# Fused attention and gated-GELU block on one core: the opening reordered around the values' weights

## The chip, the cores and the metric

The kernel runs on one core of one Trainium2 chip. The core has five engines that work side by side and meet at semaphores: TensorE (PE; its weight loads are shown apart as PEld), VectorE (DVE), ScalarE (ACT), GpSimd (POOL) and SyncE (SP, which only issues transfers here). Each engine takes its own instructions strictly in the order in which the program wrote them; one that waits holds up everything behind it on that engine. The metric is the device time of one execution in microseconds (us), the median of several.

## The reference

```python
x = A_x                                              # 1 x 2048 x 576
xn = layernorm(x)                                    # over the last axis
qkv = (xn @ wqkv).reshape(B, S, 3, 32, 18)           # 32 heads of 18
p = softmax(q @ k^T * 18 ** -0.5)
s = (p @ v).reshape(B, S, 576) @ wo
h = gelu_tanh(xn @ w_gate) * (xn @ w_up)             # 576 -> 4608
g = silu(h @ w_down)                                 # 4608 -> 576
return x + s * g
```

Everything is float32. The kernel keeps that accuracy with float16 products: each operand is split into a high and a low half (`XH`, `XL` for the normalized input; `w.hi`, `w.lo` for weights), and a product is the sum of high by high, high by low and low by high.

## The kernel before, in words

The 2048 rows are 16 tiles of 128 rows; the 576 columns are four blocks of 128 and one of 64 (the last block's high and low halves lie together in `XT`). The program has an opening, a first loop, and a long main loop.

**Weights.** `prep` turns one block of weights into its halves. Its steps are: load; largest magnitude of each of five row blocks (`amax`, DVE); the largest over all partitions (`par` to `top`); a power of two from it (`power`, `floor`, `inverse`, DVE); high halves (`split_hi`, ACT, L330); low halves (`split_lo`, on DVE where `urgent`, else on POOL). With `urgent` the largest over the partitions goes over two tiny PE products (L271, L282); otherwise it goes out to DRAM (`mxd`, L274) and comes back spread to all partitions (`mb`, L289). There is one `prep` for each of five head sets of seven heads (`j0` to `j4`, queries and keys together), one for the values (`v`), one for each of 18 gate chunks (`c0` to `c17`) and one for the output weights. The blocks that are not urgent are queued as pieces in `bg`; `subtick` takes up to three of them whenever the program calls it, as long as a budget of ACT, DVE and POOL time for that step allows.

**The opening (L1171 to L1251).** For each tile: statistics on DVE (`ln_stats`, for two or four tiles at a time, with one square root on ACT, L1141, and five small DVE steps); normalization on DVE (`ln_norm`, L1150), high half on ACT (L1154), low half on POOL (L1155, L1156); nine transpositions on PE (`ln_tr`, L1162) into PSUM (`s1` and `s2` in turn), and two copies on ACT (`ln_out`, L1167, L1168) into `XHT` and `XL`. Behind each tile stands `proj_fine`: the product of the head set `j0` with this one tile, 28 products of 128 columns (L412 to L415). After every fourth tile `evac_j` takes the two finished PSUM tiles to float16 halves (`evh` on ACT, `evl` on DVE) and stores them to DRAM in head order (`KD` from SP, `QD` from POOL for `j0`). The values' weights are loaded when tile 5 has its turn, and their pieces are dealt out over the later tiles by `V_PLAN`. After the last tile the preparations of `j1` and `c0` are queued.

**The first loop (L1442 to L1465).** `load_qk(0)` reads the first pair of heads back from DRAM (`KT`, `QT`, L1257, L1258). `qk1(0, k)`, for k from 0 to 63, is a product of one query tile with 512 keys for both heads (L1274, two matmuls that run together) and the largest of each row (L1277, DVE). Between these products PE is filled: first by the value products (`unit_v`: per tile two halves of 14 products of 288 columns, L487 to L492, taken from PSUM by ACT, L598, and stored by POOL, L612), then by `g_run`, which takes slots of a stream of paired products. A pair is 27 slots, and a slot is two matmuls on the two halves of the PE rows (L468). `pairs` gives the order of that stream: `j1`, `c0`, `c1`, `j2`, `c2`, `c3`, `j3`, and so on. 

**The main loop (from L1488).** For each of 16 pairs of heads there are 64 steps. A step has one product of the second kind (`qk2`, L1326) with its exponential (L1332), one `qk1` of the next pair, and a share of the stream's slots, of down products (L728, twelve matmuls to a stage) or of the products of probabilities and values (L1351), dealt out by `make_plan` so that all of the stream's slots are gone by the end of pair 14. Every row of `order` named below is a row of the built program.

The lines that the prediction follows most closely are these:

```python
order = [("v", spec_v) ...]                  # the stream's order
for j in units_j:
    order += [j, units_c.pop(0), units_c.pop(0)]
...
load_qk(0)
fills(9, 2.0)
while k < 64:
    if done_units[0]: qk1(0, k); subtick(FIRST); g_run(7); ...
    else:             qk1(0, k); qk1(0, k + 1); ...; fill(1.9)
```

## Time and profile before

| | |
|---|---|
| median of 3 runs | 2615.22 us (2613.48 to 2615.82) |
| the profiled execution | 2615.07 us, of which the span from first to last instruction 2613.3 us |
| busy share of the span | PE 96%, DVE 74%, ACT 64%, POOL 58% |
| first product of the first loop that has both heads | 93.98 us |
| last of its 64 products | 194.58 us |
| sixth product of the second pair (from here the main loop runs) | 216.20 us |

In the views below a row of the timeline has the start in us, the duration in us, the engine, the line, the operation, output and inputs, and in square brackets the idle time ahead of it with what ended it. Rows that PE overlaps are pipelined: the distance of two starts, not the duration, is what one matmul costs. A row of a window table has the stretch, its length, the busy time of PE, PEld, DVE, ACT and POOL with their instructions, the granted PE clock (1.00 is full speed), the busy share of the DMA engines and GB/s.

### The profile page before, as it was taken

The page shows a single profiled execution, that of the slowest core. Times are in us where ns is not written, and L with a number is a line of the kernel's source. Part 1 is how long each engine was busy: PE and PEld are TensorE (multiplying, and loading weights), DVE is VectorE, ACT ScalarE, POOL GpSimd, SP SyncE. Part 2 cuts the span into 40 slices and gives each one's busy share as a digit, 9 for nine tenths or more (in the row PEclk, how much of TensorE's full clock was granted, in tenths as well). Part 3 has the DMA queues.
Part 4 walks back from the last instruction along what each step waited for, and adds up shares of the span by engine and source line. Part 5 has one row for each costly group of instructions (what it writes and reads, how often), then busy time and mean ns, then how long its engine had stood idle before and what let it go on. Part 6 is the DMA issues. An engine that isn't in the chain of part 4 may idle for free.

```text
span 2613.3 us, 60781 instructions
## 1 busy us (share of the span) xinstructions
PE 2509.3 (96%) x25800; PEld 1326.2 (51%) x25800; DVE 1933.6 (74%) x2719; ACT 1661.2 (64%) x2081; POOL 1509.2 (58%) x1428
## 2 busy tenths in 40 slices
PE   6899999999999999999999999999999999999987
PEld 6564545455545545455555455555445444445544
DVE  7587778777877777777777778787777777777544
ACT  5225666666767666766666666767666675666663
POOL 4247663576537553757656574847666675847413
PEclk9999999999999999999999999999999999999999
DMA  4430022201120112101011120201111111100123
GB/s 144 124 113 16 12 58 63 53 18 54 34 79 19 33 31 64 45 24 51 13 53 25 23 55 11 56 9 39 28 36 26 37 29 40 38 19 6 45 72 123
DMA packets 134156, 118.68 MB, mean 45 GB/s; under 512 B 60160, under 2 KB 112792, under 8 KB 133884
## 3 DMA queue, kind: packets, MB, share of 16 engines
q1 hardware_dynamic: 128892, 105.38, 15.0%
q0 software_dynamic: 2432, 6.54, 0.7%
q8 instruction: 201, 3.29, 0.5%
q10 hardware_dynamic: 2560, 2.89, 0.3%
q14 instruction: 71, 0.58, 0.1%
HBM read 84.89 MB, written 29.61 MB: 44 GB/s over the span
## 4 chain that ended last, share of the span: by engine, by line
PE 79%; DVE 10%; ACT 4%; issue 2%; DMA 2%; POOL 2%; SPq 0%; ACTq 0%; POOLq 0%; DVEq 0%
PE mb_t L468 16%; PE ma_t L468 15%; PE md_t L728 15%; PE md_t L1351 9%; PE s L1326 8%; PE s L1274 8%; PE ma_t L1351 6%; DVE PM L1277 3%; ACT P L1332 1%; DVE osb L1359 1%; DVE m_c L248 1%; PE md_t L900 1%; PE mb_t L900 1%; PE mb_t L1351 1%; DMA QT<-QD 1%
## 5 line engine op out<-in xcount | busy, mean ns | idle before, releaser
L1277 DVE TENSOR_REDUCE PM<-s 128x2 f32<-128x1024 f32 x1024 | 1251.1, 1224 | 341.1 <-PE s L1274 332.7
L1332 ACT ACTIVATE P<-s,etab 128x1024 f32<-128x1024 f32 x896 | 996.1, 1112 | 620.5 <-PE s L1326 605.0
L468 PE MATMUL ma_t<-XHT,whi_c 64*128 64x512 f16 x1440 | 542.4, 377 | 10.5 <-DVE osb L1357 5.6
L468 PE MATMUL mb_t<-XHT,whi_c 64*128 64x512 f16 x1440 | 542.3, 377 | 3.8 <-DVE touch L436 2.0
L468 PE MATMUL ma_t<-XHT,wlo_c 64*128 64x512 f16 x1296 | 487.9, 376 | 0.0
L468 PE MATMUL mb_t<-XHT,wlo_c 64*128 64x512 f16 x1152 | 433.7, 376 | 0.0
L468 PE MATMUL ma_t<-XL,whi_c 64*128 64x512 f16 x1152 | 433.4, 376 | 0.0
L468 PE MATMUL mb_t<-XL,whi_c 64*128 64x512 f16 x1152 | 433.3, 376 | 0.0
L1274 PE MATMUL s<-KT,QT 54*128 54x512 f16 x2048 | 399.8, 378 | 20.2 <-DVE PM L1277 9.4
L1326 PE MATMUL s<-QT,KT 56*128 56x512 f16 x2048 | 405.7, 380 | 6.3 <-ACT P L1332 2.8
L468 PEld LDWEIGHTS <-whi_c 64*128 64x128 f16 x5184 | 276.7, 94 | 244.9 <-issue 29.6
L728 PE MATMUL md_t<-dhi_c,hhi 64*128 64x288 f16 x2304 | 341.6, 283 | 7.1 <-DVE osb L1359 2.2
L728 PE MATMUL md_t<-dhi_c,hlo 64*128 64x288 f16 x2304 | 341.3, 282 | 0.0
L728 PE MATMUL md_t<-dlo_c,hhi 64*128 64x288 f16 x2304 | 340.8, 282 | 0.0
L669 POOL TENSOR_SCALAR tw<-tw 128x512 f32<-128x512 f32 x144 | 91.0, 632 | 406.5 <-ACT tw L662 406.3
L728 PEld LDWEIGHTS <-hhi 64*128 64x128 f16 x4608 | 247.3, 94 | 141.0 <-issue 22.6
L1351 PE MATMUL md_t<-P,VT 128*32 128x512 f32 x2472 | 290.2, 598 | 0.3 <-ACT P L1334 0.2
L691 POOL TENSOR_TENSOR hlo<-gv,hhi 128x512 f16<-128x512 f32 x144 | 168.0, 1167 | 206.2 <-ACT hhi L684 195.5
L1326 PEld LDWEIGHTS <-KT 56*128 56x128 f16 x2048 | 125.8, 94 | 245.4 <-issue 159.2
L656 POOL TENSOR_TENSOR tw<-gs 128x512 f32<-128x512 f32 x144 | 150.6, 1046 | 140.1 <-ACT gs L633 139.7
L748 DVE SCALAR_TENSOR_TENSOR y<-md_t,c_c,y 128x576 f32<-128x576 f32 x272 | 219.2, 806 | 8.3 <-PE md_t L728 8.2
L468 PEld LDWEIGHTS <-wlo_c 64*128 64x128 f16 x2592 | 139.5, 94 | 121.5 <-issue 0.7
(260 smaller groups left out, 4075.4 us busy)
## 6 DMA issues: line engine op xcount, KB each, us to landing
draw_c<-in_B_w_down SPq DMA_DIRECT2D x18, 576.0 KB
raw_c<-in_B_w_gate SPq DMA_DIRECT2D x18, 512.0 KB
raw_c<-in_B_w_up SPq DMA_DIRECT2D x18, 512.0 KB
obr<-rd SPq DMA_DIRECT2D x30, 256.0 KB
KT<-KD SPq DMA_DIRECT2D x32, 224.0 KB
QT<-QD SPq DMA_DIRECT2D x32, 216.0 KB
VS<-vst POOLq DMA_DIRECT2D x16, 304.0 KB, 3.8
VT<-VS SPq DMA_DIRECT2D x16, 304.0 KB
```

The lines of the kernel that those rows point to most:

```text
L468: nc.tensor.matmul(o, lw, xx, start=self.stage == 0 and self.k == 0, stop=self.stage == 1 and self.k == self.slots - 1, skip_group_check=True,
L656: gp.tensor_tensor(st["t"], st["g"], st["g"], op=ALU.mult)
L669: gp.tensor_scalar(st["t"], st["t"], 1.0, 1.0, op0=ALU.mult, op1=ALU.add)
L691: gp.tensor_tensor(hs.lo[:, ft], st["v"], hs.hi[:, ft], op=ALU.subtract)
L728: nc.tensor.matmul(self.t.t[:, hf, 0:288], a[r, ft, sl], b[r, ft, 288 * hf:288 * hf + 288], start=self.stage == 0 and k == 0, stop=self.st ...
L748: nc.vector.scalar_tensor_tensor(yy, y, w.c, yy, op0=ALU.mult, op1=ALU.add)
L900: nc.tensor.matmul(o, a, b, start=self.stage == 0 and self.k == 0, stop=self.stage == 1 and self.k == len(terms) - 1, skip_group_check=True,)
L1274: nc.tensor.matmul(s1[:, h], QT[p][r, P * qt:P * qt + P], KT[p][r, 512 * kb:512 * kb + 512], start=True, stop=True)
L1277: nc.vector.tensor_reduce(PM[p][:, :, qt, kb:kb + 1], s1, op=ALU.max, axis=AX.X)
L1326: nc.tensor.matmul(s2[:, h], KT[p][r, P * kt:P * kt + P], QT[p][r, 512 * qb:512 * qb + 512], start=True, stop=True)
L1332: nc.scalar.activation(pt, s2, AF.Exp, scale=ETAB[j0])
L1351: nc.tensor.matmul(t.t[qd:qd + 32, :], VT[p][:, c0:c0 + 32], pt[:, h], start=kt == k0, stop=kt == k1, skip_group_check=True,)
```

## The change

The change rewrites the opening and the order of the stream; the main loop's code stays.

- **Values first.** The values' weights are loaded first (in five pieces, into buffers that the pairs of heads use later) and prepared first, ahead of `j0`. Value products are then written tile by tile between the transpositions: `value()` writes the 28 products of one tile. Twelve of the 16 tiles are so written before the first loop instead of the 147 products (five tiles and a quarter) that stood there. An even tile's two halves go to one two-bank PSUM tile (`s2`) and are taken by one ACT instruction. The transpositions use `s1` alone.
- **First heads by groups of four tiles.** `proj_fine` is gone. `j0` is computed by `unit_j` as the other head sets are: per group of four tiles one pair of 27 slots with 512 columns, written in two halves (`half_pair`, 14 and 13 slots) between the tiles. The last slot of a first half reads `XU`, a copy of part of `XHT` to other partitions by a transfer from SP.
- **Statistics by groups.** `ln_stats` has one piece for each tile, one for the square root and one for the rest; groups of four tiles are written as a block (`run(g2)`, `run(g3)`).
- **Two head sets ahead of the gates.** The stream's order is `j1`, `j2`, `c0`, `c1`, `j3`, ... Their weights (and those of `c0`) are queued during the opening (`start_first`); `j2` gets buffers of its own. From the last transposition until `load_qk(0)` nothing is taken from `bg` (`hold`). In the first loop `g_run` takes 7 slots a step until `v`, `j1` and `j2` are done, then 4.
- **Queues.** The query halves of `j1` and `j2` are stored from POOL too (`j <= 2`). The loads of x stay as they were: four single tiles from ACT, the rest from SP.

The diff, cut to its core:

```diff
-        while bg and n < most:
+        while bg and n < most and not hold[0]:
...
-            q = nc.gpsimd if j == 0 and part == 0 else nc.sync
+            q = nc.gpsimd if j <= 2 and part == 0 else nc.sync
...
+            if early[0] and st % 2 == 0:
+                both = ps.tile([P, 2, 512], F32, tag="s2", name=f"v{st}")
...
+    order.append(units_j.pop(0))
     for j in units_j:
         order += [j, units_c.pop(0), units_c.pop(0)]
...
-    def ln_out(st):
-        sl = slice(P * st, P * st + P)
-        tp = tps[st]
-        nc.scalar.activation(XHT[:, :, sl], tp[:, 0, 0:640].rearrange("p (a b) -> p a b", a=5), AF.Copy)
-        nc.scalar.activation(XL[:, :, sl], tp[:, 1, 0:512].rearrange("p (a b) -> p a b", a=4), AF.Copy)
-
-    def proj_fine(st):
...
+        def spread_out():
+            nc.scalar.activation(XHT[:, :, sl], tp[:, 0, 0:640].rearrange("p (a b) -> p a b", a=5), AF.Copy)
+            nc.scalar.activation(XL[:, :, sl], tp[:, 1, 0:512].rearrange("p (a b) -> p a b", a=4), AF.Copy)
+            if st % 4 == 3:
+                cols = slice(P * st - 384, P * st + P)
+                nc.sync.dma_start(XU[64:128, cols], XT[0:64, cols])
...
+    def value(n=1):
+        for _ in range(28 * n):
+            next(vgen)
+        subtick(dict(FREE, T=3.4 * n))
...
+    def half_pair():
+        if not jpair:
+            jpair.append(next(jgen))
+        u = jpair[0]
+        u.begin()
+        while not u.slot():
+            pass
+        if u.stage == 2:
+            jpair.clear()
+        subtick(dict(FREE, T=2.9))
...
+        value()
+        run(g2)
+        transposed(5)
+        for st in range(8, 12):
+            ln_norm(st)
+        half_pair()
+        transposed(6)
+        value()
+        run(g3)
+        transposed(7)
...
+        transposed(15)
+        hold[0] = True
+        half_pair()
+        value()
+        half_pair()
+        filler[0] = vgen
...
-    filler[0] = unit_v(preps[0])
     load_qk(0)
-    fills(9, 2.0)
+    hold[0] = False
+    for _ in range(2):
+        value()
+    early[0] = False
...
-            g_run(7)
+            g_run(7 if done_units[0] < 3 else 4)
```

How the order moves is shown at three places. The first is PE at the start, from the last of the second tile's transpositions (`tp`). Before, `j0`'s products with single tiles follow:

```order
L1162 LDWEIGHTS xn_135
L1162 MATMUL tp_193<-ident,xn_135 128x128
L412 LDWEIGHTS whi_j_190
L412 MATMUL ma_t<-XHT,whi_j_190 126x128
L412 LDWEIGHTS whi_j_190
L412 MATMUL ma_t<-XL,whi_j_190 126x128
```

Now value products follow:

```order
L1242 LDWEIGHTS xn_151
L1242 MATMUL tp_217<-ident,xn_151 128x128
L507 LDWEIGHTS XHT
L507 MATMUL v_253<-whi_v,XHT 128x288
L507 LDWEIGHTS XHT
L507 MATMUL v_253<-wlo_v,XHT 128x288
```

So the first product after the second tile's transpositions now waits for the values' halves instead of `j0`'s.

The second place is ACT around the square root for tiles 8 to 11 (`sd`). `vst` are value halves taken from PSUM, `hi_j` and `whi_j` the high halves of `j0`'s weights, `evh` those of finished head tiles, `xn` the high half of a normalized tile; before, the same square root stands between single tiles:

```order
L1154 ACTIVATE xn_422<-xt 128x576
L1141 ACTIVATE sd_313<-mv,epst 128x4
L1167 ACTIVATE XHT<-tp_380 128x5x128
L1168 ACTIVATE XL<-tp_380 128x4x128
L514 ACTIVATE evh_1_0_442<-ma_t 126x512
L514 ACTIVATE evh_0_0_444<-mb_t 126x512
```

Now it stands behind `j0`'s high halves and the fourth value tile, and ahead of the copies of tile 5 (`tp_501`):

```order
L1245 ACTIVATE XHT<-tp_408 128x5x128
L1246 ACTIVATE XL<-tp_408 128x4x128
L349 ACTIVATE hi_j_426<-raw_j_116,s_j_423 128x252 x5
L633 ACTIVATE vst_446<-mc_t 128x16x18
L633 ACTIVATE vst_446<-pv_t 128x16x18
L1222 ACTIVATE sd_482<-mv,epst 128x4
L1245 ACTIVATE XHT<-tp_501 128x5x128
L1246 ACTIVATE XL<-tp_501 128x4x128
L1233 ACTIVATE xn_514<-xt 128x576
```

So the copies of tile 5, and with them the one PSUM tile that all transpositions now use, wait for the statistics of tiles 8 to 11.

The third place is SP where the first heads come back from DRAM, behind the last stores of keys. Before, the loads of `j1`'s raw weights stand between:

```order
L534 DMA KD_370<-evh_1_3_1052 7x18x512
L229 DMA raw_j_1066<-in_A_wqkv 128x4x126
L233 DMA raw_j_1066<-in_A_wqkv 128x1x126
L229 DMA raw_j_1066<-in_A_wqkv 128x4x126
L233 DMA raw_j_1066<-in_A_wqkv 128x1x126
L1257 DMA KT_1075<-KD_370 56x2048
L1258 DMA QT_1074<-QD_369 54x2048
```

Now the read-back follows at once, and two spread loads of weight maxima stand behind it:

```order
L554 DMA KD_534<-evh_1_3_1207 7x18x512
L1363 DMA KT_1220<-KD_534 56x2048
L1364 DMA QT_1219<-QD_533 54x2048
L1363 DMA KT_1220<-KD_534 56x2048
L1364 DMA QT_1219<-QD_533 54x2048
L305 DMA mb_j_1264<-mxd_j_910 128x128
L305 DMA mb_j_1264<-mxd_j_1002 128x128
```

The raw weights of `j1` and `j2` have moved to the middle of the opening on the same queue.

More of the change, by code (lines that the diff above doesn't have):

```diff
@@ L130 @@
     bg = deque()
+    hold = [False]
     class Gate:
@@ L257, in small @@
         def small(nm):
-            return stage.p.tile([P, 512], F32, tag="pv", name=nm)
+            return ps.tile([P, 512], F32, tag="ma", name=nm)
         def par():
@@ L365, in prep @@
         act, dve = on_act(), on_dve()
-        low_cost = [dve if urgent or t in vec else on_pool(2.75) for t in range(5)]
+        low_cost = [dve if t in vec else on_pool(2.75) for t in range(5)]
         rest(1.9 * lead)
         add(load)
-        rest(13.0)
+        if not urgent:
+            pieces.append(Rest(13.0, lambda: w.loaded))
         for t in range(5):
@@ L1241 @@
-        while pv0:
-            pv0.popleft()()
-        start_prep(1)
-        start_prep(2)
-        for _ in range(3):
-            subtick()
+        tile0 = ln_tr(0)
+        run(sb[1:3] + pv0[1:3] + sb[3:])
+        tile0()
+        ln_norm(2)
+        ln_norm(3)
+        run(pv0[3:])
+        transposed(1)
+        run(pj0[1:6] + g1[:4])
+        value()
+        transposed(2)
+        value()
+        run(pj0[6:7])
+        run(g1[4:])
+        transposed(3)
+        ln_norm(4)
+        run(pj0[7:8])
@@ new lines @@
+        value()
+        for st in (5, 6, 7):
+            ln_norm(st)
+        transposed(4)
+        run(pj0[8:])
+        start_first()
+        value()
+        run(g2)
+        transposed(5)
+        for st in range(8, 12):
+            ln_norm(st)
+        half_pair()
+        transposed(6)
+        value()
+        run(g3)
+        transposed(7)
+        ln_norm(12)
+        ln_norm(13)
+        half_pair()
+        transposed(8)
+        ln_norm(14)
+        half_pair()
+        transposed(9)
```

236 lines of the change are left out of this document (137 added, 99 removed).

## The prediction

> **What bounds the kernel now.** I read the busy shares first, then windows over the stages, then PE's timeline in the opening.
>
> ```profile
> PE 2509.3 (96%) x25800; PEld 1326.2 (51%) x25800; DVE 1933.6 (74%) x2719; ACT 1661.2 (64%) x2081; POOL 1509.2 (58%) x1428
> ```
>
> ```profile
> 0.00:20.00 20.00, 5.28 (x33) 3.59 (x33) 12.72 (x43) 8.05 (x15) 5.06 (x14) 1.00 0.80 271
> 80.00:100.00 20.00, 11.23 (x67) 6.49 (x65) 5.00 (x9) 1.64 (x4) 1.96 (x5) 0.74 0.45 123
> 900.00:1100.00 200.00, 195.50 (x1902) 96.42 (x1904) 155.07 (x210) 131.51 (x153) 103.97 (x96) 0.99 0.18 47
> ```
>
> PE bounds the main loop (195.50 of 200 us busy). So work that PE does before it is worth its full PE price later, and every us that PE stands in the opening is lost. It stands there in two stretches: until it has something to multiply, and around 90 us. The second is this one:
>
> ```profile
> 67.38 0.29 PE L487 MATMUL ma_t<-whi_v,XHT 128*128 128x288 f16 x1
> 85.19 0.39 PE L1274 MATMUL s<-KT,QT 54*128 54x512 f16 x1 [0.38 <-DMA QT<-QD]
> 93.98 1.03 PE L1274 MATMUL s<-KT,QT 54*128 54x512 f16 x3 [8.39 <-DMA QT<-QD]
> ```
>
> `j0`'s last product ends at 67.38; its heads come back from DRAM, and the first product with both starts at 93.98. The value products written between last only to 85.
>
> My yardstick is the sixth product of the second pair of heads: from there both programs run the same loop. Before, it is at 216.20:
>
> ```profile
> 194.58 0.40 PE L1274 MATMUL s<-KT,QT 54*128 54x512 f16 x2
> 214.25 0.40 PE L1274 MATMUL s<-KT,QT 54*128 54x512 f16 x2
> 215.98 0.40 PE L1326 MATMUL s<-QT,KT 56*128 56x512 f16 x2
> 216.20 0.40 PE L1274 MATMUL s<-KT,QT 54*128 54x512 f16 x2
> ```
>
> From 214.25 to 215.98 there are one such product (0.22, the distance 215.98 to 216.20) and seven slots: a slot is 1.51/7 = 0.216.
>
> **The change, part by part.** *What is ahead at the yardstick.* Counted in the two built orders, 223 of the stream's 4320 slots (`j0` not among them) stand before it now and 328 after the change, and one down stage. That is 105 x 0.216 = 22.7, and six distances of 288 columns, 0.7: 23.4 us less for a main loop that PE bounds. Prices of the rest:
>
> ```profile
> 63.66 0.67 PE L1162 MATMUL tp<-ident,xn 128*128 128x128 f16 x9
> 64.16 0.22 PE L412 MATMUL mc_t<-XHT,whi_j 128*126 128x128 f16 x1
> 65.77 0.22 PE L412 MATMUL mc_t<-XHT,whi_j 128*126 128x128 f16 x1
> 80.37 0.29 PE L487 MATMUL mc_t<-whi_v,XHT 128*128 128x288 f16 x1
> 82.08 0.29 PE L487 MATMUL pv_t<-whi_v,XHT 128*128 128x288 f16 x1
> ```
>
> A tile's transpositions cost 0.5. `j0` with one tile costs 1.61 (65.77 to 67.38), 25.8 for 16; as four pairs it is 108 slots, 23.3, so 2.5 less. Half a value tile is 1.71, a tile 3.43.
>
> *Start.* DVE now needs the third tile's statistics ahead of the first scales, and the values' maxima ahead of any product:
>
> ```profile
> 5.00:6.00 1.00, 0.00 (x0) 0.00 (x0) 0.59 (x3) 0.00 (x0) 0.00 (x0) 1.00 0.98 336
> 12.24 0.16 DVE L262 TENSOR_REDUCE mx_j<-m_j 128x1 f32<-128x5 f32 x1
> 14.76 0.15 DVE L312 TENSOR_SCALAR s_j<-s_j 128x1 f32<-128x1 f32 x1
> 20.38 0.81 DVE L1129 BATCH_NORM_STATS2 st<-xt 128x6 f32<-128x288 f32 x2
> 24.14 0.53 DVE L1150 TENSOR_SCALAR xt<-xt,mv,rs_all 128x576 f32<-128x576 f32 x1
> L1150 DVE TENSOR_SCALAR xt<-xt,mv,rs_all 128x576 f32<-128x576 f32 x16 | 11.7, 735 | 0.1
> L248 DVE TENSOR_REDUCE m_v<-raw_v 128x1 f32<-128x576 f32 x5 | 3.5, 724 | 0.0
> L330 ACT ACTIVATE whi_v<-raw_v,s_v 128x576 f16<-128x576 f32 x5 | 3.8, 775 | 0.0
> ```
>
> Four tiles of statistics take 3.76 (20.38 to 24.14), one 0.94. At some 336 GB/s, with transfers starting near 2 us and half the share, the third tile of 295 kB is there at about 7.3; the values' 1.47 MB by 10. From 7.3 DVE has two tiles of statistics (1.9), two groups of small steps (0.8 each, five steps of 0.16), four normalizations at 0.53 (they range up to the mean of 0.735), a small copy, five maxima at 0.7, and the last maximum: 9.4, so 16.7. From there to the scale took `j0` 2.7 (12.24 to 14.91): 19.4; one high half 0.8: first value product at 20.2. Five low halves at about 0.75 pace the first half tile; the second runs near the end of the slow clock: first tile done at 26.2.
>
> *PE up to the end of the eighth half pair.* Nine value tiles and six products more (31.6), 14 tiles of transpositions (7.0), 108 slots (23.3), two tiny products (1.1): 63.0, so 89.2 without waits. Now the waits. ACT's prices:
>
> ```profile
> 18.27 1.68 ACT L330 ACTIVATE whi_j<-raw_j,s_j 128x252 f16<-128x252 f32 x4
> 36.18 0.70 ACT L1154 ACTIVATE xn<-xt 128x576 f16<-128x576 f32 x1
> 36.75 0.72 ACT L1167 ACTIVATE XHT<-tp 128x640 f16<-128x640 f16 x1
> 37.34 0.63 ACT L1168 ACTIVATE XL<-tp 128x512 f16<-128x512 f16 x1
> 37.81 0.72 ACT L1154 ACTIVATE xn<-xt 128x576 f16<-128x576 f32 x1
> ```
>
> A high half of x is 0.57, the two copies of a tile 1.06, a high half of `j0` 0.42.
> (a) `mb_j` on PE stands ahead of the third value tile and needs a DVE step behind tile 4's normalization, behind the scales, behind a square root that ACT has behind the second tile's values. PE is free at 26.2 + 0.5 + 3.4 + 0.5 + 0.5 = 31.1, DVE done at 32.5: 1.4.
> (b) The transpositions of tile 6 need the one PSUM tile that ACT empties of tile 5, and that copy stands behind the square root for tiles 8 to 11. ACT from the third value tile's end at 36.7: value copy 0.7, three high halves 1.7, copies of tile 4 1.1, five halves of `j0` 2.1: 42.3. DVE: last low half 0.4, four tiles of statistics 3.8: 46.5; square root 0.3, copies 1.1: 47.9. PE is through tile 4's and 5's transpositions, the fourth value tile and 14 slots at 44.1: 3.8 of waiting.
> (c) The seventh half waits for copies of tile 15: about 0.5. Elsewhere the copies keep ahead: in the 14 tiles after the second, ACT needs some 45 us of 75.
> So 5.7, and the eighth half ends at 94.9. The added DMA of `XU` reaches its slot 2.8 after it is issued at the earliest, and I take it as hidden behind the 13 slots ahead of it; uncovered it would cost up to 3 at four places.
>
> *Read-back.* What was removed from SP's queue, `j1`'s raw loads, now runs in the middle of the opening.
>
> ```profile
> 78.75 0.32 SPq L1258 DMA_DIRECT2D QT<-QD  x1
> 94.53 0.41 SPq L1257 DMA_DIRECT2D KT<-KD  x1
> 101.00:102.00 1.00, 1.00 (x10) 0.49 (x7) 0.67 (x1) 0.00 (x0) 0.59 (x2) 1.00 0.11 25
> DMA to landing us min/median/max: 2.8/3.6/6.2
> ```
>
> After the last product come two ACT and two DVE steps (2.0), three stores from POOL (0.6 each, the last issued at +2.4 to +3.0), landing 3.6 later (the last row is that of the stores to `QD`): +6.7. Loads of this size for the second pair, issued from 94.53, were through when DMA fell silent at about 101.1: 6.6. So +13.3, first product at 108.2. It is bounded by +10 (each landing at its lowest) and +22: the first pair's last load was issued at 78.75 and landed 15.2 later. I take the 6.6, since the raw loads that ran beside the slow one are gone, though three value stores remain. 50 value products (6.1) cover part; PE stands 7.2.
>
> *First loop.*
>
> ```profile
> 101.58 0.61 PE L1274 MATMUL s<-KT,QT 54*128 54x512 f16 x4
> 106.82 0.60 PE L1274 MATMUL s<-KT,QT 54*128 54x512 f16 x4
> 162.10 0.37 PE L468 MATMUL pv_t<-XHT,whi_j 64*126 64x512 f16 x1 [0.65 <-DVE touch L436]
> 169.66 0.37 PE L468 MATMUL mb_t<-XHT,whi_j 64*126 64x512 f16 x1 [0.64 <-DVE touch L436]
> L1277 DVE TENSOR_REDUCE PM<-s 128x2 f32<-128x1024 f32 x1024 | 1251.1, 1224 | 341.1 <-PE s L1274 332.7
> ```
>
> Sixteen products beside the last 112 value products: 5.24 for four (101.58 to 106.82) with 31 of them, so 21.0 less 1.5 for 12 missing, plus 2.7 for 5.4 us at half clock (below): 22.2. Thirty-two beside `j1` and `j2`: eight pairs at 7.56 (162.10 to 169.66): 60.5, and 2.0 for `c0`'s maxima, which DVE must take there. Sixteen with four slots (1.08 of PE): DVE sets 1.22 each, 19.5. From the last one to the yardstick it took 21.6 with 67 slots; now 58 and the stage: 20.4. Together 124.6: yardstick at 232.8, 16.6 later.
>
> *The sum:* 16.6 lost, 23.4 gained, 6.8 net. The profiled execution had 2615.07, which is 0.15 under the median: 2608.4 there, 2609 to hold against the median.
>
> A weighed rule, on the clock:
>
> ```profile
> 88.00:90.00 2.00, 0.00 (x0) 0.00 (x0) 0.00 (x0) 0.00 (x0) 0.00 (x0) 0.78 0.01 2
> 98.00:100.00 2.00, 2.00 (x12) 0.69 (x10) 0.69 (x1) 0.00 (x0) 0.00 (x0) 0.66 0.77 193
> ```
>
> PE's last product before the gap ended at 85.58 and the clock halved near 89.1 (0.78 is the mean of 88 to 90), 3.5 later; work began at 93.98 and full speed was back near 99.4, 5.4 later. The wait (b) of 3.8 is just over that. In the sum I leave its clock at full; halved, it would cost 5.4/2 = 2.7, and the sum would be 2612.
> The Trainium skill, in "TensorE: Matmul & The Clock Gate", Part 1 (the HAM clock gate), says that one idle window of about 3.4 us, free-running, halves the clock and that as long a busy one brings it back; the fall here agrees (3.5), the return took longer. By the page's figure the drop would cost an estimate of 1.7, and the sum would be 2611.
>
> **The rivals.** *The read-back stays slow:* if the load takes 15.2 as at 78.75, the first product comes 8.6 later: 2617, no change. For it: value stores are in flight beside it in both orders. Against: the raw loads are gone.
> *PE's clock and DVE's groups feed each other, and it gets slower.* The place is the copies of tiles 5 and 7, each behind a square root that waits for four tiles of statistics. The drop at (b) costs 2.7; a like wait at tile 7, where I find PE and ACT within 0.5 of each other, costs 3.8 + 2.7; normalizations at their mean of 0.735 instead of 0.53 add 12 x 0.2 = 2.4. Together 11.6: 2620. Above 6.8 of it the change loses; above 12 it is slower by over 0.2%. For it: those rows leave no slack. Against: the copies cost ACT 1.06 a tile, and PE has 3 to 7 us of work between two of them.
> The clock-gate page of the Trainium skill speaks for this rival, since it asks for no idle gap over 3.4 us.
> *The waits are smaller:* without (a) and (b), 5.2 less, and with the eight pairs at their PE price (4 x 0.22 + 27 x 0.216 = 6.7 instead of 7.56), 6.9 less: 2597. Against: DVE is as loaded there as before.
> *The slots ahead aren't worth their price,* as the main loop partly waits for DVE: at half, 2620. Against: 195.50 of 200.
>
> **How the numbers follow.** Within 0.2% (5.2 us) of 2615.2 counts as no change; that is about what a measurement of this kernel can tell. My sum, with an own range of 2603 to 2614: 0.37, three quarters of it below 2610. Slow read-back 0.20, all in the middle. Clock and groups 0.22, 2615 to 2625, most of it slower. Smaller waits 0.15, faster. Slots not worth it 0.06, slower. Faster 0.28 + 0.15 = 0.43; same 0.09 + 0.20 + 0.04 = 0.33; slower 0.24. The range 2597 to 2623 leaves some two in ten out.
>
> **What would show it.** First value product at 20.2; PE idle for 1.4 ahead of the third value tile and 3.8 ahead of tile 6's transpositions; eighth half done near 95; first product of the first pair near 108 with PE idle for 7 ahead of it; the 64th 104 later; yardstick near 233. I am wrong if the halved clock shows in windows of the opening beyond its first 6 us, if the first product comes after 115, or if the main loop from the yardstick to the end (2397 now) isn't some 23 shorter.

## The result, and the profile after

The changed kernel took 2655.61 us (median of 4 runs, 2651.24 to 2659.2), the kernel before 2614.9 beside it: a ratio of 1.0156, with a 95% interval of 1.0144 to 1.0169. It is 41 us slower, where 2609 was forecast and 2623 was the end of the range.

The profiled execution took 2654.63 us, its span 2652.8. First the changed kernel's busy shares and granted clock, and below them the granted clock of the kernel before:

```profile
PE 2516.5 (95%) x25568; PEld 1322.0 (50%) x25568; DVE 1930.6 (73%) x2714; ACT 1663.3 (63%) x2075; POOL 1528.7 (58%) x1452
core 0: 2652.8 us, clock 0.986
```

```profile
core 0: 2613.3 us, clock 0.994
```

PE has 232 matmuls fewer and is busy for 7 us longer: it ran more of them at half clock. (The 232 are the change itself: `j0` took 16 x 28 = 448 products with single tiles, and takes 4 x 27 x 2 = 216 in four pairs.) 0.014 of 2652.8 us is 37 us of full speed not granted; before it was 0.006 of 2613.3, 16 us.

Next, PE's timeline at the steps of the prediction, in the changed kernel:

```profile
21.54 0.40 PE L507 MATMUL v<-whi_v,XHT 128*128 128x288 f16 x1 [0.56 <-ACT whi_v L349]
33.65 0.38 PE L297 MATMUL mb_j<-m_j,ones 1*128 1x1 f32 x2 [1.37 <-DVE m_j L295]
49.71 1.12 PE L1242 MATMUL tp<-ident,xn 128*128 128x128 f16 x9 [4.43 <-ACT XL L1246]
60.61 0.37 PE L488 MATMUL ma_t<-XHT,hi_j 64*126 64x512 f16 x1 [1.22 <-DVE evl L539]
101.82 0.38 PE L488 MATMUL ma_t<-XHT,hi_j 64*126 64x512 f16 x1
116.25 0.60 PE L1380 MATMUL s<-KT,QT 54*128 54x512 f16 x1 [7.83 <-DMA QT<-QD]
118.36 1.03 PE L1380 MATMUL s<-KT,QT 54*128 54x512 f16 x3 [1.50 <-DMA QT<-QD]
253.14 0.40 PE L1380 MATMUL s<-KT,QT 54*128 54x512 f16 x2
```

The eighth half pair ends at 102.0 (94.9 was forecast), the first product with both heads is at 118.36 (108.2), and the yardstick, the sixth product of the second pair, at 253.14 (232.8; before 216.20). From there to the end of the span it is 2399.7 us, where the kernel before needs 2397.1: not 23.4 shorter but 2.6 longer. So of the 46 us between forecast and result 20 arose ahead of the yardstick and 26 behind it. These are the windows from the yardstick to the end, first of the kernel before, then of the changed one:

```profile
216.20:2613.30 2397.10, 2333.82 (x24165) 1201.31 (x24161) 1780.13 (x2462) 1586.83 (x1941) 1420.60 (x1302) 1.00 0.15 39
253.14:2652.80 2399.66, 2319.95 (x23943) 1188.44 (x23939) 1771.36 (x2423) 1583.17 (x1928) 1416.67 (x1292) 0.99 0.14 37
```

The work did move: 222 matmuls fewer are left, which are the two of each of the 105 slots and the twelve of the down stage. But PE's busy time fell by only 13.9 us instead of 23.4, and its idle time rose from 63.3 to 79.7 us. The 26 us are thus 16.4 of waiting and 9.5 of matmuls that ran slower.

Behind it, this is where PE waits in the main loop (260 to 2480; who waited for what: us in total, times, longest), the costliest group of each kernel. The kernel before:

```profile
PE s L1274 <- DVE PM L1277: 7.9, 8, 2.1
```

and the changed kernel:

```profile
PE s L1432 <- DMA QT<-md: 12.7, 6, 4.5
```

A wait for `QT<-md` is new. In all, the rows of these two views add up to 35.3 us of waiting before and 51.3 after. At the border between two pairs the row maxima of the next pair go out to DRAM (`md<-rms`) and come back as two rows of `QT`, both issued by ACT; the first product of the next pair needs them. This is one such border in the kernel before, ACT's timeline and its window (length; busy us and instructions of PE, PE's weight loads, DVE, ACT and POOL; granted clock, DMA share, GB/s):

```profile
659.03 0.46 ACTq L1300 DMA_DIRECT2D md<-rms  x1
661.34 0.54 ACTq L1304 DMA_DIRECT2D QT<-md  x2
```

its window:

```profile
658.00:664.00 6.00, 5.90 (x61) 3.23 (x59) 4.43 (x5) 4.01 (x6) 0.92 (x2) 1.00 0.04 8
```

and the same border in the changed kernel, from SP's, ACT's and PE's timelines and the window:

```profile
688.64 0.41 SPq L244 DMA_DIRECT2D raw_c<-in_B_w_gate  x1
691.08 3.40 SPq L256 DMA_DIRECT2D draw_c<-in_B_w_down  x1
691.36 0.46 ACTq L1406 DMA_DIRECT2D md<-rms  x1
696.73 0.54 ACTq L1410 DMA_DIRECT2D QT<-md  x2
701.45 0.92 PE L1432 MATMUL s<-QT,KT 56*128 56x512 f16 x2 [3.95 <-DMA QT<-md]
```

its window:

```profile
690.00:700.00 10.00, 7.50 (x83) 4.20 (x79) 5.29 (x8) 5.53 (x8) 2.92 (x4) 1.00 0.79 212
```

Before, the DMA engines are nearly idle at this border (share 0.04) and the first step comes back after 2.31 us. Now a gate set's weights are on their way (share 0.79), the first step takes 5.37, the second is late too, and PE stands 3.95 us. The border at 994 looks the same (2.87). A slow first step alone isn't enough: in the kernel before it took 4.95 us at 504 and 5.30 at 1853, beside other transfers (DMA share 0.51 and 0.72), and PE waited for no `QT<-md` there. At 691 the load is still running behind the second step too. The Trainium skill, in "DMA: Bandwidth & Descriptors", section "Issuing engines are not separate DMA queues", says that transfers issued by different engines run on the same 16 DMA engines and interleave; these rows agree, since the slow transfers are ACT's and the load is SP's.

In the middle of a pair the same load meets the sums' way through DRAM (`sd`, `oc`, `rd`, `obr`). DVE's and PE's timelines of the changed kernel, where a load issued at 499.69 stands ahead of `obr` (502.89):

```profile
512.84 0.69 DVE L1506 TENSOR_TENSOR osb<-osb,obr 128x512 f32<-128x512 f32 x1 [4.49 <-DMA obr<-rd]
514.72 0.61 PE L1380 MATMUL s<-KT,QT 54*128 54x512 f16 x2 [4.05 <-DVE touch L456]
```

its window:

```profile
513.00:521.00 8.00, 6.28 (x32) 2.66 (x33) 4.77 (x6) 3.27 (x4) 1.89 (x2) 0.57 0.01 2
```

DVE stands in its own order for a transfer, PE stands behind DVE (for the small step `touch`), and the clock falls behind it (0.57 in the last row). At the last border but one (2337) it is the output weights' maxima on DVE (`m_wo`) that stand ahead of the burst's sum `osb`, and the largest wait for `QT<-md` follows:

```profile
2334.14 1.39 DVE L263 TENSOR_REDUCE m_wo<-raw_wo 128x1 f32<-128x576 f32 x2
2335.65 0.68 DVE L1465 TENSOR_TENSOR osb<-md_t,osb 128x512 f32<-128x512 f32 x1
2336.38 0.26 PE L1402 MATMUL md_t<-ident,rmc 128*64 128x128 f16 x1 [2.43 <-DVE osb L1465]
2348.64 0.61 PE L1432 MATMUL s<-QT,KT 56*128 56x512 f16 x1 [4.46 <-DMA QT<-md]
```

So 5.1 of the 12.7 us (4.46, and 0.63 right behind it) are of another kind: no weight load is issued there. Between the two steps, issued at 2336.99 and 2344.30, the DMA share is 0.04, and still the first step took 7.31 us. The one transfer issued shortly ahead of it is the store of the same maxima (`mxd_wo`, from SP at 2335.76); in the kernel before, whose border is at 2305.73, that store can only follow the reduction of these maxima at 2328.6. The second step then ran beside two more transfers from SP (`mb_wo` at 2343.40, `VT` at 2343.83). Why the first was so slow, no run shows.

### The profile page after: what moved, and what is told of

It is laid out like the page before. It is cut to its first block, busy times and chain, and to the rows that moved or that the text cites. A ratio compares the mean times of both kernels' runs of the same rounds, so it can differ in the third digit from the quotient of the medians.

```text
span 2652.8 us, 60346 instructions
## 1 busy us (share of the span) xinstructions
PE 2516.5 (95%) x25568; PEld 1322.0 (50%) x25568; DVE 1930.6 (73%) x2714; ACT 1663.3 (63%) x2075; POOL 1528.7 (58%) x1452
## 4 chain that ended last, share of the span: by engine, by line
PE 74%; DVE 9%; POOL 6%; DMA 4%; ACT 3%; issue 3%; SPq 1%; ACTq 0%; POOLq 0%; DVEq 0%
PE mb_t L488 14%; PE md_t L762 14%; PE ma_t L488 14%; PE md_t L1457 9%; PE s L1432 7%; PE s L1380 7%; PE ma_t L1457 5%; DVE PM L1383 4%; ACT P L1438 1%; POOL raw_c L356 1%; PE md_t L934 1%; DMA md<-rms 1%; DMA QT<-md 1%; DVE osb L1465 1%; POOL wlo_c L357 1%
## 5 line engine op out<-in xcount | busy, mean ns | idle before, releaser
L1432 PE MATMUL s<-QT,KT 56*128 56x512 f16 x2048 | 407.6, 381 | 20.6 <-DMA QT<-md 12.7
L1457 PE MATMUL md_t<-P,VT 128*32 128x512 f32 x2752 | 319.8, 596 | 1.1 <-DVE osb L1465 0.8
L1380 PEld LDWEIGHTS <-QT 54*128 54x128 f16 x2048 | 140.2, 96 | 123.2 <-issue 37.3
```

Source lines behind the costliest of these rows:

```text
L1380: nc.tensor.matmul(s1[:, h], QT[p][r, P * qt:P * qt + P], KT[p][r, 512 * kb:512 * kb + 512], start=True, stop=True)
L1432: nc.tensor.matmul(s2[:, h], KT[p][r, P * kt:P * kt + P], QT[p][r, 512 * qb:512 * qb + 512], start=True, stop=True)
L1457: nc.tensor.matmul(t.t[qd:qd + 32, :], VT[p][:, c0:c0 + 32], pt[:, h], start=kt == k0, stop=kt == k1, skip_group_check=True,)
```

## The experiments

My theory after these rows: the slots ahead were worth their price, but the change moved the stream against the pairs' borders, so that big loads now run beside small round trips; at the last border but one the output weights' maxima do harm; and in the first loop DVE is the bound. The rival for the first half: DVE and the planner set these waits, and the loads only stand beside them. Times are medians with the ratio to the kernel before measured beside them. That kernel itself came out between 2612.80 and 2615.45 us beside them, so where runs were not made together the ratios decide.

**The loads kept clear of the round trips.** A gate ahead of a set's load lets it go only from the fifth to the fiftieth step of a pair and while no sum is on its way.

```diff
+        if name not in ("v", "j0", "j1", "j2", "c0", "c1"):
+            pieces.append(Gate(lambda: 4 <= place[0] < 50 and not dividing[0]))
         add(load)
-            pieces.append(Rest(13.0, lambda: w.loaded))
+            pieces.append(Rest(MAXIMA.get(name, 13.0), lambda: w.loaded))   # wo: 50
...
+            dividing[0] += not last      # where a sum starts; -1 behind obr
...
+            place[0] = i                 # each step of a pair
```

> The changed kernel, but a set's weight loads (from the third gate set and the fourth head set on) are issued only when no row maxima and no sums are on their way through DRAM; and the output weights' maxima wait until the last pair's border is past. Theory A (the main loop lost its gain because the big loads now meet the small round trips, PE and DVE wait for those, and the clock halves behind each wait): the waits for QT<-md of 3.95, 2.87 and 4.46 us, those behind the DVE's wait for obr and oc (4.05 and 2.25) and that for osb at 2336 (2.43) go, 20 us, and about 27 us of half clock with them, worth 10: 2625, anywhere from 2620 to 2637. Theory B (DVE and the planner set these waits, the loads only stand beside them): the waits return at other places, 2648 to 2660.

Measured: 2650.17 us, 1.0137 (1.0122 to 1.0152). By the time that is theory B, whose range begins at 2648. But the course is theory A's at first. By the moments when a pair's maxima go out (`md<-rms`), the run was 39 us behind the kernel before at the first of these sixteen moments and 26 at the eighth, where the changed kernel went from 37 to 47. From there it lost again, at waits that neither kernel had (8.86 us here, 6.19 at 2000):

```profile
1393.24 0.42 PE L767 MATMUL md_t<-dhi_c,hhi 64*128 64x288 f16 x2 [8.86 <-DVE touch L461]
```

I took it that the gate had made the later sets' loads so late that the program, written in planned time, waited for weights. Then the mechanism stands for the first half of the loop, and my remedy has a cost of its own. This run alone can't tell that from theory B, so I limited the gate.

**Only the early sets kept clear.**

```diff
-        if name not in ("v", "j0", "j1", "j2", "c0", "c1"):
+        if name in ("j3", "j4", "c2", "c3", "c4", "c5", "c6", "c7", "c8"):
```

> As the run with the loads kept clear, but only for the third to ninth gate set and the fourth and fifth head set: there the weights still come in time, while in that run the later loads came so late that PE stood 8.86 us at 1393 and 6.19 us at 2000 for a down stage. The output weights' load is left where the changed kernel has it, their maxima still wait until the last border is past. Theory A (loads beside the small round trips cost the middle of the main loop its gain): up to the ninth pair as in that run, 26 us behind the kernel before instead of 45, from there the changed kernel's own course (16 us gained until the last pair), and no 10 us lost at the last border: 2620 to 2635. Theory B (the later loss in that run was the same loss in another place): again 2645 or more.

Measured: 2626.77 us, 1.0042 (1.0027 to 1.0057): 28.8 us less than the changed kernel, in theory A's range. The load of that border now goes out behind `obr`, 25 us past it (the maxima go out at 685.82; the rows are of SP's timeline), the round trip has PE wait no longer, and this is the yardstick, the window from it to the end, and what is left of the wait for `QT<-md`:

```profile
710.70 0.55 SPq L1509 DMA_DIRECT2D obr<-rd  x1
711.34 0.43 SPq L247 DMA_DIRECT2D raw_c<-in_B_w_gate  x1
```

```profile
255.49 0.40 PE L1385 MATMUL s<-KT,QT 54*128 54x512 f16 x2
255.49:2624.70 2369.21, 2307.65 (x23943) 1191.96 (x23939) 1774.82 (x2423) 1580.92 (x1928) 1413.85 (x1292) 1.00 0.14 38
PE s L1437 <- DMA QT<-md: 2.1, 2, 1.8
```

From the yardstick at 255.49 there remain 2369.2 of 2624.7 us, 27.9 fewer than in the kernel before. With the same 23943 matmuls as in the changed kernel, PE is busy for 26.2 us less than before and idle for 1.7 less (all waits of the view together 34.4). So the slots ahead were worth the 23.4 of the prediction, and a little more, once the loads and the output weights' maxima were out of the way. Nothing ahead of the yardstick had become better.

The 28.8 us have two parts, since the edit moves two things. When the maxima go out for the fourteenth time, the run is 15.9 us behind the kernel before and the changed kernel 31.3: 15.4 us come up to there, where only the loads were moved. At the sixteenth time it is 11.7 against 39.6: another 12.5 come with the output weights' maxima, which in the changed kernel stand ahead of the fifteenth round trip (the one at 2337). One wait for `QT<-md` above 1 us is left (1.83 at 1284), and there a load that was not gated goes out 4.6 us ahead of the maxima. The gate was not tried in the kernel before, but that kernel has no wait for `QT<-md` to lose.

**The same collision made in the kernel before.** Four gate sets' loads are held until the row maxima go out.

```diff
+        if name in ("c4", "c6", "c13", "c14"):
+            pieces.append(Gate(lambda: place[0] >= 60 and sent[0] == place[1] + 1))
+            add(follow)                  # a store of one element of rms
         add(load)
```

> The kernel before, with the loads of four gate sets (c4, c6, c13, c14) held until the row maxima of the next pair go out to DRAM, so that they run beside that round trip; a store of one element is added ahead of each. Theory A: four new waits for QT<-md of 2.5 to 4.5 us and a halved clock of 3.4 us behind each, 4.5 to 6 us a border, 18 to 25 in all: 2633 to 2640. Theory B: the round trip has room, no wait over 1 us for QT<-md, 2613 to 2619.

Measured: 2618.63 us, 1.0012 (1.0003 to 1.0021); the wait at the first of the borders, and ACT's two issues there:

```profile
658.89 0.46 ACTq L1309 DMA_DIRECT2D md<-rms  x1
661.20 0.54 ACTq L1314 DMA_DIRECT2D QT<-md  x2
666.71 0.82 PE L1336 MATMUL s<-QT,KT 56*128 56x512 f16 x2 [2.28 <-DMA QT<-md]
```

The waits are there, 2.28, 2.03 and 1.04 us, but the time is theory B's, and much cheaper than theory A had it. The first step took 2.31 us, as before, though the load was issued 0.31 us behind it; only the second was late. So I issued the loads 1.3 to 2.1 us sooner, ahead of the store of the maxima, towards where the changed kernel had them.

```diff
-            pieces.append(Gate(lambda: place[0] >= 60 and sent[0] == place[1] + 1))
+            pieces.append(Gate(lambda: place[0] >= 58 and sent[0] == place[1] + 1))
...
+            sent[:] = p, ...             # now behind rmc, not behind md<-rms
```

> The kernel before, with the loads of the same four gate sets issued as soon as the row maxima of the next pair are split, some 2 us ahead of their store to DRAM, as the changed kernel had it at 688 and 990 (loads issued behind that store cost 2.28 us of waiting at one border, 2.03 at another, 1.04 at a third, and 3 to 4 us in all). Theory A (it counts that both steps of the round trip run beside the load): waits of 3 to 4 us at three or four borders with the clock halved behind them, 10 to 18 us over the kernel before, 2625 to 2633. Theory B (a border has some 3 us of slack whatever runs beside it): no more than 5 us, 2620 or less.

Measured: 2631.84 us, 1.0061 (1.0044 to 1.0078): 16.4 us slower than the kernel before.

```profile
657.88 0.51 ACTq L1310 DMA_DIRECT2D md<-rms  x1
663.84 0.54 ACTq L1314 DMA_DIRECT2D QT<-md  x2
668.66 0.96 PE L1336 MATMUL s<-QT,KT 56*128 56x512 f16 x2 [5.24 <-DMA QT<-md]
```

its window:

```profile
667.00:675.00 8.00, 6.34 (x40) 4.36 (x40) 2.96 (x3) 3.55 (x7) 2.30 (x4) 0.57 0.09 22
```

Theory A holds by the time (2625 to 2633), with waits that are longer and fewer than it had them: the first step takes 5.96 us instead of 2.31, PE stands 5.24, and the clock is halved for most of the next 8. Two of the four borders pay that (the other wait is 4.85 at 1723), and one has 1.21 us. At the one at 961 (set `c6`) PE waits only 0.21 us for `QT<-md`, but 2.88 just ahead of it for a step of ACT (`gs`) that stood on ACT behind the same transfer. Between 1.3 and 2.1 us in the issue of four loads, unchanged in size, decide over 13 us of the kernel.

**Two trials on the run with the loads kept clear.** The second gate set's load 30 us later; and the copies of tile 5 ahead of the square root.

```diff
-        rest(1.9 * lead)
+        rest(1.9 * lead + 30.0 * (name == "c1"))
```

> The run with the loads kept clear, and besides the second gate set's load 30 us of planned time later, so that its seven maxima (4.3 us of DVE between 220.8 and 232.6 in the changed kernel) leave the first loop. Theory A (DVE bounds the end of the first loop, and has room in the main loop): the second pair's first product 4 us earlier, and the end 4 us below the run with the loads kept clear. Theory B (the main loop is as short of DVE): the end within 1.5 us of that run.

```diff
-        run(g2)
         transposed(5)
+        run(g2)
```

> The run with the loads kept clear, and besides the two copies of tile 5 are written ahead of the statistics and the square root of tiles 8 to 11. Theory A (this square root held the copies, as the prediction's wait (b) has it): the wait of 4.4 us ahead of tile 6's transpositions and the 3.4 us of half clock behind it go, the first product of the first pair comes 6 us earlier (110 instead of 116), and the end is 6 below the run with the loads kept clear. Theory B (the normalizations of tiles 8 to 11, now later, make the next tiles wait instead): the first product within 2 us of 116.

Measured: 2652.88 us, 1.0138 (1.0123 to 1.0153), and 2653.44, 1.0149 (1.0132 to 1.0166), against 2650.17: neither gained. The first was 6 us ahead of its base when the first maxima went out, as theory A has it, and gave it back where PE waited for the low halves that now came too late. In the second the same wait stood one tile further on, now ahead of tile 7, and the first product came at 116.27, as theory B has it:

```profile
316.57 0.60 PE L493 MATMUL ma_t<-XHT,wlo_c 64*128 64x512 f16 x1 [7.07 <-POOL wlo_c L360]
```

```profile
53.82 0.91 PE L1247 MATMUL tp<-ident,xn 128*128 128x128 f16 x7 [4.49 <-ACT XL L1251]
```

In that run ACT's square root still waits 3.59 us for DVE's statistics (`mv`). So it is those that are late, and not the order of ACT's two instructions. Both trials were made again in a better form, on the run with the early sets kept clear:

```diff
+        run(g2[:4])          # statistics, while DVE stands
         run(pj0[8:])
         start_first()
         value()
-        run(g2)
+        run(g2[4:])
```

> The run before this one, and the statistics of tiles 8 to 11 are written ahead of the first heads' scale and split, their square root and scales behind it (DVE stands idle from 35.7 to 41.5 in the changed kernel). Theory A (the square root waits for four tiles of statistics that DVE does too late): the 4.4 us ahead of a transposition near 50 and the half clock behind it go, first product of the first pair near 110, end 5 to 6 us below that run. Theory B (the copies are late for ACT's own load): the wait stays above 3 us, first product within 2 of 116.

Measured: 2626.18 us, 1.004 (1.0025 to 1.0055), 0.6 from its base. The 4.4 us ahead of the transposition are gone, as theory A has it, but 2.58 us for the next pair's `evl` take their place, and the first product behind the read-back is at 114.20 instead of 115.48, which is theory B's time. With the second gate set's load 16 us later on top of that:

```diff
-        rest(1.9 * lead)
+        rest(1.9 * lead + 16.0 * (name == "c1"))
```

> The run before this one, and the second gate set's load 16 us of planned time later (30 made PE wait 7.07 us at 316 for its low halves, which took back the 6 us gained by then). Theory A (DVE bounds the end of the first loop and has room later): the second pair's first maximum 4 to 6 us earlier and the end 4 to 6 below the run before this one. Theory B (the main loop is as short of DVE): the end within 1.5 us of it.

Measured: 2616.79 us, 1.0006 (0.9996 to 1.0015): 9.4 us below the run before it, more than theory A had, and no longer to be told from the kernel before. Where the time was, in the changed kernel: the second gate set's maxima (the view of the tile `m_c`), the window, and the same part of this run:

```profile
L263 DVE TENSOR_REDUCE m_c<-raw_c x5: 662/678/680, 220.8 to 227.8; 128x1 f32<-128x512 f32 x5
L268 DVE TENSOR_REDUCE m_c<-draw_c x2: 744/744/744, 230.1 to 231.9; 128x1 f32<-128x576 f32 x2
```

its window:

```profile
212.00:234.00 22.00, 17.16 (x132) 7.70 (x131) 21.27 (x27) 5.08 (x7) 10.82 (x12) 0.92 0.25 74
```

```profile
206.00:230.00 24.00, 20.11 (x175) 9.50 (x173) 22.64 (x26) 6.46 (x10) 17.99 (x20) 1.00 0.49 129
```

and the timeline:

```profile
244.00 0.39 PE L1386 MATMUL s<-KT,QT 54*128 54x512 f16 x2
```

DVE was busy for 21.27 of 22 us; PE stood for it, and ran at 0.92 of its clock. In this run DVE is hardly less busy (22.64 of 24), but the clock is full, and the yardstick comes at 244.00 instead of 253.14 (253.64 in the run before this one). The seven maxima are 4.9 us of DVE by their medians (5 x 0.678 and 2 x 0.744); the rest of the 9.4 I put down to the lower clock behind the waits that they made, which no run shows by itself.

**Four more, on that last run.**

> The run with the second gate set's load 16 us later, but the query stores of the second and third head set issued from SP as before, not from POOL. Theory A (the prediction costed this part at nothing): end within 2 us of that run. Theory B (on POOL they delay the gate set's low halves, 1.9 us for each of four groups): 3 to 6 us below it.

The edit is `j == 0` for `j <= 2` in the choice of the store queue. Measured: 2618.46, 1.0016 (1.0007 to 1.0025), against 1.0006 (0.9996 to 1.0015) of its base: not below it but, if anything, above. So theory B falls, and the stores from POOL cost nothing, as predicted.

The statistics of tiles 12 to 15 later:

```diff
-        run(g3)
         transposed(7)
-        ln_norm(12)
-        ln_norm(13)
         half_pair()
         transposed(8)
-        ln_norm(14)
+        run(g3[:2])
         half_pair()
         transposed(9)
-        ln_norm(15)
+        run(g3[2:4])
         value()
+        run(g3[4:])
...
```

> The run with the second gate set's load 16 us later, and in the opening the statistics, scales and normalizations of tiles 12 to 15 are written later, behind the low halves of the first pair of heads. Theory A (in that run PE stands 2.59 us at 55.9 for the low half evl, which DVE has behind four normalizations and four tiles of statistics, and runs at half clock for 3.4 us from 56.0): both go, the first pair's first product 3 to 4 us earlier than 113.0, and the end 3 to 4 below that run: 2613. Theory B (DVE has as much to do either way, and the copies of later tiles are late instead): first product within 1.5 us of 113, end within 1.5 of that run.

Measured: 2614.11, 1.0005 (0.9996 to 1.0014). The wait at 56 and its half clock are gone (the window 48 to 64 has a clock of 1.00 and PE busy 14.68 of 16), the first product behind the read-back is at 111.54 instead of 113.02, 1.48 sooner. The whole is 2.7 below its base by the medians, but so is the kernel before beside it (2612.80 against 2615.45); by the ratios, 1.0005 and 1.0006, nothing is gained. That is theory B: the wait went, and the end did not follow.

The sets in their old order:

```diff
-    order.append(units_j.pop(0))
...
-        for i in (1, 2, 3):
-            start_prep(i, ps)
...
+        start_prep(1)
+        start_prep(2)
...
-            g_run(7 if done_units[0] < 3 else 4)
+            g_run(7 if done_units[0] < 2 else 2)
```

> The run with the second gate set's load 16 us later, but with the sets in the order of the kernel before (one head set, two gate sets, then the next head set), the opening as in the changed kernel; with the first loop at 2 slots a product once the gate set has begun, since more finds no room there. Theory A (the second head set is what covers the preparation of the first gate set's weights, which took from the load at 139 to the last low half at 204.8, and it is work done beside DVE's maxima): PE stands some 20 us near 180 to 200 for the first low halves, and 86 fewer slots (18.6 us) are done by the second pair, against some 11 us less of first loop: 2635 to 2650. Theory B (the order brings nothing by itself): 2613 to 2622.

Measured: 2672.96, 1.0225 (1.0211 to 1.0239), worse than both theories. The part that was asked for is there, PE waits for the first gate set's halves (4.81 us at 187.25) and runs at half clock for 17 us, as its window shows:

```profile
187.00:204.00 17.00, 10.88 (x48) 2.72 (x50) 6.64 (x7) 3.98 (x7) 16.20 (x12) 0.51 0.18 53
```

But the run also stood 9.97 us at 91 in the opening and waited for late weights at 783 and 1085, so it doesn't settle what the order is worth by itself.

Last, the gap of the read-back filled: four value tiles there instead of two, on the run with the later statistics.

```diff
-    for _ in range(2):
+    for _ in range(4):
         value()
...
-            g_run(7 if done_units[0] < 3 else 4)
+            g_run(7 if done_units[0] < 3 else 3)
...
-        rest(6.5)
+        rest(6.5 + 6.0 * (name == "j3"))
```

> The run with the statistics of tiles 12 to 15 moved, and: four value tiles instead of two between the read-back's issue and the first pair's first product (PE stands 7.93 us there and runs at half clock from 106.1 to 119.8), 3 slots instead of 4 a product at the end of the first loop, which now has 24 such products, and 6 us more of planned time for the broadcast of the fourth head set's maximum (PE stands 2.76 us at 346.9 behind it). Theory A (the gap and the half clock behind it are PE time that work can fill): the two tiles cost 6.9 us less later, 13.7 us of half clock shrink to under 7, the wait at 347 goes, 3 to 9 us below the run it is built on: 2605 to 2611. Theory B (DVE's maxima set the first loop from its first product on, so PE time before it buys nothing): 2612 to 2617.

Measured: 2615.83, 1.0 (0.9991 to 1.0009), in theory B's range. The gap is filled, 2.19 us of waiting are left; and what it gave was lost 35 us later, where PE stood 6.56 us behind DVE, and DVE 6.79 for a store of `evl` that shares the DMA engines with the loads of that moment:

```profile
112.17 0.60 PE L1388 MATMUL s<-KT,QT 54*128 54x512 f16 x3 [2.19 <-DMA QT<-QD]
```

```profile
146.07 0.69 DVE L544 SCALAR_TENSOR_TENSOR evl<-pv_t,evh 126x512 f16<-126x512 f32 x1 [6.79 <-DMA KD<-evl]
```

That it is a load that slows this store is argued from the timeline; no run took the load away. Theory B's reason, DVE's maxima, is not shown by it either. No version beat the kernel before by more than can be measured.

## Why the prediction was wrong, point by point

- **"23.4 us less for a main loop that PE bounds": this step failed, by 26 us.** Its price was right: with nine sets' loads and the output weights' maxima moved, the loop from the yardstick is 27.9 us shorter than before. What failed is the premise that the rest of the loop stays as it was: PE waited 16.4 us more and ran 9.5 us' worth slower. I read 195.50 of 200 busy as "PE bounds it", and didn't ask what keeps the other 4.5 small. It is a matter of phase. In the kernel before, no weight load of the main loop is issued within 12 us ahead of a border's round trip; in the changed one two are, their last transfers 0.3 and 0.7 us ahead, and a third 6. Moving 105 slots forward, and a head set in the order, moved the loads against the borders, and the output weights' maxima against the one at 2337 (12.5 of the 28.8 us). The slack of these round trips was never bounded in my sum. My rival "the slots aren't worth their price" had the right place and the wrong cause (DVE's share), half the size and a chance of 0.06.
- **First loop, 124.6 forecast, 134.8 measured.** Counted on PE's timeline, the 17th product starts at 141.38, the 49th at 209.07 and the 64th at 232.08. The value part took 23.0 for 22.2 (118.36 begins at half clock). The 32 products beside `j1` and `j2` took 67.7 for 62.5: I had put 2.0 us for the first gate set's maxima, which take 4.9 on DVE like the second's, and PE has waits of 1.8 to 2.5 at the pairs' switches, the one of 2.49 at 188 with a halved clock behind it (0.50 from 190 to 192). From the 49th to the 64th it took 23.0 for 19.5: the second gate set's maxima weren't in the sum at all. From there it was 21.1 for 20.4. Moving those maxima gave 9.4 us.
- **Opening.** The waits (a) and (b) were right, 1.37 for 1.4 and 4.43 for 3.8. In (b) I chose to leave the clock at full; it was halved from about 49.5 to 52.9 (the clock is 0.91 over the window 40 to 60). So a term for it belonged into the sum, of 1.7 us (half of 3.4) rather than the 2.7 priced beside it. Not seen were the start (21.54 for 20.2) and the wait for `evl` (1.45 with its second half); wait (c), 0.5, did not come. Together the eighth half pair was 7.1 late. These terms make 4.6 of it; the other 2.5 I put down to the switches between half pairs, tiles and transpositions, and no single row shows them.
- **Read-back.** 16.4 us from the last product to the first with both heads instead of 13.3, within its bounds (10 to 22). That is about a third of what the rival of a slow read-back had (8.6).
- **The clock and DVE's groups.** This rival was the right kind, waits that halve the clock, but I put it in the opening alone. The 21 us of full speed that the changed kernel went without beyond the kernel before (37 against 16) are spread over the opening, the first loop and the main loop.
- **Right:** the transfer of `XU` stayed hidden, the stores moved to POOL cost nothing, and all three signs named for being wrong were there: half clock at 50 us, a first product at 118, a main loop not 23 shorter.

In the sum: 20.3 late at the yardstick (7.1 + 3.0 + 10.2) and 26.0 of the main loop are the 46.3 between forecast and result of the profiled execution (2615.07 less 6.8 is 2608.3, which the prediction has as 2608.4; measured 2654.6).

## What to carry to other kernels

Before work is moved ahead of a tuned loop, list the small transfers that its borders wait for and the moments when the big ones are issued, since a shift of the whole stream changes which of them meet; a busy share of 98% doesn't show how little slack these round trips have. Where a program is written out in planned time, give big loads a place (behind the last small transfer of a chain) rather than the next free moment, but check that the data still come in time. And count the DVE work that a new order puts beside a stage which DVE already bounds, because a wait that it makes can cost PE again in clock.

## What the runs showed of the hardware that was not expected

The clock fell behind waits that were well under the 3.5 us that it took in the kernel before. One place in the changed kernel, the wait on PE's timeline and the window behind it:

```profile
802.48 0.39 PE L1380 MATMUL s<-KT,QT 54*128 54x512 f16 x2 [2.25 <-DVE touch L456]
```

its window:

```profile
803.00:807.00 4.00, 4.00 (x26) 1.76 (x24) 2.86 (x3) 1.27 (x2) 0.00 (x0) 0.60 0.10 27
```

In the kernel before, a wait of 2.05 us at 2212 left the clock at 1.00:

```profile
2212.35 0.39 PE L1274 MATMUL s<-KT,QT 54*128 54x512 f16 x2 [2.05 <-DVE PM L1277]
```

its window:

```profile
2212.00:2216.00 4.00, 3.65 (x34) 1.95 (x34) 2.89 (x4) 1.43 (x2) 0.00 (x0) 1.00 0.01 4
```

So two waits of nearly the same length differ: one costs some 1.6 us more (0.40 of the 4 us of the window), the other nothing; what decides it these runs don't show. The Trainium skill, in "TensorE: Matmul & The Clock Gate", Part 1, has it that an idle window of about 3.4 us, which runs freely, halves the clock; the wait of 2.25 us doesn't agree with that. And after the long gap of the read-back, with PE only half busy, the clock was at half for 12 us on end:

```profile
112.00:124.00 12.00, 6.24 (x24) 2.62 (x24) 2.42 (x3) 0.41 (x1) 0.00 (x0) 0.50 0.66 199
```
